# A ring tile for two batches, and a reordered prologue, in a Fourier mixer followed by an expert block

## The chip, the cores and the metric

One core of a Trainium2 chip. The metric is the device time of one execution in microseconds; a time quoted is the median of several runs. The kernel is bound by TensorE (PE) for all but its first 42 us. In the profile's lines PE is TensorE, DVE is VectorE, ACT is ScalarE, POOL is GpSimd ("Pool" in the text) and SP is SyncE; a line starts with the start and the length in us, L265 is line 265 of that run's kernel, and the bracket gives the idle time of the engine before it and what the profile says ended it. "Half clock" means that the granted TensorE clock is 0.5.

## The reference

```python
X = np.fft.rfft(x, axis=1)                    # x: 8 batches x 3008 positions x 256
Y = X * (filt_r + 1j * filt_i)[None]
y = np.fft.irfft(Y, n=3008, axis=1)
h = y.reshape(8 * 3008, 256) @ w_in           # 256 x 2048
out = np.maximum(0.01 * h, h) @ w_out         # 2048 x 256
```

## The kernel before

The transform of 3008 = 94 x 32 points is done as matmuls in two stages each way: S1 (by 94), a transpose T1 on VectorE, S2 (by 32), a product with the filter, SA (inverse of S2), a transpose T2, SB (inverse of S1), which leaves the mixer output with channels on partitions. The expert block runs in 47 chunks of 512 tokens. Batches 1 to 7 are mixed in the shadow of the expert matmuls. Batch 0 has nothing to hide behind: its mixing is the prologue. "The first expert matmul" below is the first one of `moe1_group`.

The two tiles of mixer output and the chunk that straddles a batch boundary:

```python
yts = [cpool.tile([P, NDT, N], FP16, name=f"yt{i}") for i in range(2)]
...
    while t < (ci + 1) * CH:                       # moe1_group
        e = min((ci + 1) * CH, (t // N + 1) * N)   # cut at each batch boundary
        pieces.append((t // N, t % N, t - ci * CH, e - t))
        t = e
    for j in range(2):
        for b, lo, o, ln in pieces:
            for dt in range(NDT):
                nc.tensor.matmul(ph[:, j, ds(o, ln)], w_in_sb[...], yts[b % 2][:, dt, ds(lo, ln)], ...)
```

PSUM tiles are taken in turn: two wide ones (two banks each, kind "ph"), three single ones ("pf"). An S2 group of batch 0 handles `n` values of k1 of one half `hf` of the channels; VectorE or Pool multiplies it by both filters, into y tiles that SA reads:

```python
def bank(kind, n, w):
    of = wide if kind == "ph" else single
    t = of[turn[kind] % len(of)]; turn[kind] += 1
    ...
def first_s2(hf, c, n, on_pool):
    ps = bank("ph", n, DH)
    ...                                # matmuls into ps
    if on_pool:                        # ScalarE copies ps to SBUF, Pool multiplies
        ...
    else:
        y = [ypp.tile([P, n, DH], FP16, tag=f"yw{i}", bufs=2, ...) for i in range(2)]
        for i in range(2):             # by the real filter fa, then by the imaginary fb
            nc.vector.tensor_tensor(y[i][:], ps, fs[i], AL.mult)
def first_sa(hf, c):                   # per four k1: two matmuls into a single bank,
    ps = bank("pf", 4, DH)             # then a ScalarE copy to big[2]
```

The prologue's order from T1 on (program order is each engine's order):

```python
t1_part(0, 0, True)(), t1_part(0, 1, True)()
upper(0)                               # copies of filter halves, ScalarE and VectorE
first_s2(0, 0, 8, False)
first_s2(0, 8, 8, True)
x_load(1)                              # next batch, Pool queue
t1_part(0, 2, True)()
keep_warm(4)                           # filler matmuls on an idle tile
first_s2(0, 16, 4, False)
first_s2(0, 20, 4, True)
t1_part(0, 3, True)()
first_sa(0, 0), first_sa(0, 16)
keep_warm(3)
first_s2(1, 0, 8, False)
first_s2(1, 8, 8, True)
first_sa(0, 8), first_sa(0, 20)
keep_warm(2)
...                                    # load of w_out
first_s2(1, 16, 8, False)
first_sa(1, 0)
keep_warm(4)
first_t2(0), first_t2(1)
first_sa(1, 16), first_sa(1, 8)
first_t2(2), first_t2(3)
```

Before all this Pool's queue gets the loads of x, twelve filter loads, the inverse constants `i1` (wanted by SB) and `w_in`.

## Time and profile before

| | before |
|---|---|
| time, first 3 runs | 783.31 us (783.25 to 783.39) |
| profiled run | 783.91 us, span 782.1 us |
| end of the first two T1 transposes | 20.45 us |
| start of T2 | 34.67 us |
| first expert matmul | 42.48 us |
| PE busy after that, to 771.5 | 728.10 of 729.02 us |

Two quantities matter: how long the chain from T1 to the first expert matmul is (42.48 - 20.45 = 22.03 us), and the PE work after it. I count from the end of T1 because the loads before it land up to a microsecond earlier or later from run to run.

### The profile page before, as it was taken

The numbers are of one execution on the slowest core, as the hardware profiler recorded it, in microseconds if no ns is written. First come the engines' busy times: TensorE is split into PE (matmuls) and PEld (weight loads), VectorE is DVE, ScalarE is ACT, GpSimd is POOL, SyncE is SP. The second block draws the span as 40 slices with busy tenths as digits, with TensorE's granted clock in tenths as the row PEclk, the third lists the DMA queues.
The fourth block names the chain that finished last, engine by engine and source line by source line (L and its number), as shares of the span: only waits on it lengthen the run. The fifth ranks groups of instructions, "written<-read, shape, count | busy, mean of one in ns | idle before, by whom it ended". The sixth has DMA issues, their size and how long they took to land.

```text
span 782.1 us, 13672 instructions
## 1 busy us (share of the span) xinstructions
PE 773.4 (99%) x5844; PEld 531.4 (68%) x5844; DVE 367.3 (47%) x462; ACT 551.2 (70%) x784; POOL 152.3 (19%) x126
## 2 busy tenths in 40 slices
PE   9899999999999999999999999999999999999998
PEld 4366677666776667766777667776677666776666
DVE  3879751865237641577307754087432765200000
ACT  3686769676787767777587775967668776666664
POOL 5963300340004300052001510025000340000000
PEclk9999999999999999999999999999999999999999
DMA  9963102301041101510105010140101001101111
GB/s 179 226 110 73 38 28 56 94 27 42 28 108 41 41 28 41 108 42 28 42 28 121 28 37 32 42 107 28 41 28 41 28 28 41 41 33 35 41 41 54
DMA packets 39387, 44.16 MB, mean 56 GB/s; under 512 B 11266, under 2 KB 37506, under 8 KB 38658
## 3 DMA queue, kind: packets, MB, share of 16 engines
q0 software_dynamic: 13136, 17.78, 13.3%
q1 hardware_dynamic: 26192, 25.53, 9.3%
q8 instruction: 45, 0.74, 0.4%
q14 instruction: 14, 0.11, 0.0%
HBM read 35.67 MB, written 24.64 MB: 77 GB/s over the span
## 4 chain that ended last, share of the span: by engine, by line
PE 94%; DMA 2%; POOL 2%; ACT 1%; DVE 1%; issue 1%; POOLq 0%
PE ph L376 41%; PE po_ps L390 41%; PE pf L176 3%; PE pf L243 2%; PE pf L231 2%; PE pf L216 2%; DMA fb_sb<-in_filt_i_dram 2%; PE pf L390 1%; POOL fy_h_c L276 1%; ACT big L187 0%; POOL x_sb L132 0%; DVE big L297 0%; ACT big L290 0%; POOL fb_sb L140 0%; ACT gt_c L381 0%
## 5 line engine op out<-in xcount | busy, mean ns | idle before, releaser
L381 ACT ACTIVATE gt_c<-ph 128x1024 f16<-128x1024 f32 x376 | 384.8, 1023 | 195.7 <-PE ph L376 194.7
L376 PE MATMUL ph<-yt,w_in_sb 128*128 128x512 f16 (+7 forms) x1728 | 386.7, 351 | 0.3
L390 PE MATMUL po_ps<-w_out_sb,gt_c 128*128 128x256 f16 x2944 | 381.4, 272 | 0.6 <-ACT ost_c_t L397 0.6
L390 PEld LDWEIGHTS <-gt_c 128*128 128x128 f16 x3008 | 290.7, 98 | 87.1 <-issue 1.9
L376 PEld LDWEIGHTS <-w_in_sb 128*128 128x128 f16 x1728 | 162.9, 98 | 94.4 <-issue 0.4
L224 POOL TENSOR_TENSOR y_b_g<-p_b_g,p_b_g 128x512 f16<-128x512 f32 x84 | 106.9, 1272 | 225.4 <-DVE p_b_g L222 225.4
L199 DVE STREAM_TRANSPOSE big<-big 128x1024 f32<-128x1024 f32 x32 | 55.9, 1847 | 126.2 <-ACT big L187 126.2
L187 ACT CAST big<-pf 128x512 f16<-128x512 f32 x186 | 106.6, 604 | 1.7 <-PE pf L256 1.7
L246 DVE CAST yt<-pf 128x376 f16<-128x376 f32 x112 | 56.3, 544 | 86.0 <-PE pf L243 86.0
L220 DVE TENSOR_TENSOR p_b_g<-pf,fa_sb 128x512 f32<-128x512 f32 x84 | 58.1, 692 | 38.1 <-PE pf L216 35.6
L397 ACT COPY ost_c_t<-po_ps 128x256 f32<-128x256 f32 x184 | 69.4, 377 | 6.6 <-PE po_ps L390 5.4
L207 DVE STREAM_TRANSPOSE big<-big 128x1024 f32<-128x1024 f32 x28 | 51.1, 1934 | 34.1 <-ACT big L187 34.1
L221 DVE TENSOR_TENSOR p_b_g<-pf,fb_sb 64x512 f32<-64x512 f32 x84 | 58.2, 692 | 1.1
L222 DVE TENSOR_TENSOR p_b_g<-pf,fb_sb 64x512 f32<-64x512 f32 x84 | 57.4, 683 | 1.1
L132 POOL DMA_DIRECT2D x_sb<-in_x_dram x12 | 6.6, 553 | 253.3 <-PE pf L176 252.5
L243 PEld LDWEIGHTS <-big 128*128 128x128 f16 x448 | 25.6, 98 | 13.2
L176 PE MATMUL pf<-x_sb,f_sb 94*128 94x256 f16 x224 | 33.9, 272 | 0.2 <-DVE yt L246 0.2
L231 PE MATMUL pf<-y_b_g,small_sb 128*128 128x512 f16 x84 | 31.8, 379 | 0.0
L216 PE MATMUL pf<-big,small_sb 128*128 128x512 f16 x84 | 31.8, 379 | 0.0
L243 PE MATMUL pf<-i_sb,big 128*128 128x94 f16 x448 | 28.6, 206 | 0.0
L176 PEld LDWEIGHTS <-f_sb 94*128 94x128 f16 x224 | 20.9, 97 | 9.1 <-issue 0.4
L318 PE MATMUL po_ps<-idle 128*128 128x512 f16 x72 | 19.5, 418 | 1.2 <-DVE one L165 1.2
(46 smaller groups left out, 158.8 us busy)
## 6 DMA issues: line engine op xcount, KB each, us to landing
out_dram<-ost_c_t SPq DMA_DIRECT2D x92, 256.0 KB, 2.1
x_sb<-in_x_dram POOLq DMA_DIRECT2D x6, 1536.0 KB, 11.4
x_sb<-in_x_dram POOLq DMA_DIRECT2D x3, 480.0 KB, 9.8
fa_sb<-in_filt_r_dram POOLq DMA_DIRECT2D x6, 192.0 KB, 10.2
fb_sb<-in_filt_i_dram POOLq DMA_DIRECT2D x6, 192.0 KB, 8.5
w_in_sb<-in_moe_w_in_dram POOLq DMA_DIRECT2D x1, 1024.0 KB, 13.0
w_out_sb<-in_moe_w_out_dram POOLq DMA_DIRECT2D x1, 1024.0 KB, 13.0
x_sb<-in_x_dram POOLq DMA_DIRECT2D x1, 1024.0 KB, 7.9
```

Source lines behind the costliest of these rows:

```text
L176: nc.tensor.matmul(ps[:, j, :], f1_sb[:N1, n2, :], x_sb[:N1, n2, :], start=True, stop=True)
L187: copy(paired(dst)[:, ds(n0, nn), ds(e0, de)], ps.rearrange("p n (e t) -> p n e t", t=2))
L220: nc.vector.tensor_tensor(p1[:], ps, fa, AL.mult)
L221: nc.vector.tensor_tensor(p2[0:64], ps[64:P], fb[64:P], AL.mult)
L222: nc.vector.tensor_tensor(p2[64:P], ps[0:64], fb[0:64], AL.mult)
L224: nc.gpsimd.tensor_tensor(y1[:], p1[:], p2[:], AL.add)
L243: nc.tensor.matmul(ps[:, j, :], src[:, dt, n2, :], i1_sb[:, n2, :], start=True, stop=True)
L246: copy(yv[:, :, ds(4 * h, 4)], ps.rearrange("p c a -> p a c"))
L376: nc.tensor.matmul(ph[:, j, ds(o, ln)], w_in_sb[:, dt, ts(ct, P)], yts[b % 2][:, dt, ds(lo, ln)], start=(dt == 0), stop=(dt == NDT - 1),)
L381: nc.scalar.activation(gts[ci][:, ds(2 * g, 2), :], ph, AF.Lrelu)
L390: nc.tensor.matmul(po, gts[ci][:, ct, ts(tj, P)], w_out_sb[:, ct, :], start=(ct == 0), stop=(ct == NCT - 1))
L397: nc.scalar.copy(ost[:, tj % 2, :], po)
```

## The change

Intent: one tile for two batches, so that half of the straddling chunks need no cut; and a prologue in which Pool multiplies earlier, fewer engines wait on each other, and the load of the constants leaves Pool's queue.

```diff
-    yts = [cpool.tile([P, NDT, N], FP16, name=f"yt{i}") for i in range(2)]
+    yt = cpool.tile([P, NDT, 2 * N], FP16, name="yt")
...
-    nc.gpsimd.dma_start(i1_sb[:], i1_d.ap())
-    nc.gpsimd.dma_start(w_in_sb[:], ...)
...
-        ps = bank("ph", n, DH)
+        ps = bank(two[n // 8], n, DH)          # groups of four: a single bank
...
     t1_part(0, 0, True)(), t1_part(0, 1, True)()
+    nc.vector.memset(i1_sb[:, 0, 0:2], 0.0)    # holds the load back until T1 is done
+    nc.sync.dma_start(i1_sb[:], i1_d.ap())
     upper(0)
+    first_s2(0, 8, 8, True)
+    nc.gpsimd.dma_start(w_in_sb[:], ...)
+    t1_part(0, 2, True)()
     first_s2(0, 0, 8, False)
... (old order removed)
+    keep_warm(3)
+    first_s2(0, 20, 4, True)
+    for n0 in (0, N2 // 2):
+        x_load(1, n0, N2 // 2)
+    t1_part(0, 3, True)()
     first_s2(0, 16, 4, False)
+    first_s2(1, 0, 8, False)
+    first_sa(0, 0)
+    first_s2(1, 8, 8, True)
+    first_sa(0, 16)
+    first_s2(1, 16, 4, False)
+    first_sa(0, 8)
+    ... (load of w_out)
+    first_s2(1, 20, 4, False)
+    first_sa(1, 0), first_sa(0, 20)
     keep_warm(3)
     first_t2(0), first_t2(1)
+    first_sa(1, 16), first_sa(1, 20), first_sa(1, 8)
     first_t2(2), first_t2(3)
...
-            e = min((ci + 1) * CH, (t // N + 1) * N)
+            e = min((ci + 1) * CH, (t // (2 * N) + 1) * 2 * N)
```

More of the change, by code (lines that the diff above doesn't have):

```diff
@@ L158 @@
     filt_load(fb_sb, filt_i, DH, DH, 64)
-    nc.gpsimd.dma_start(i1_sb[:], i1_d.ap())
-    nc.gpsimd.dma_start(w_in_sb[:], moe_w_in.rearrange("(dt p) c -> p dt c", p=P))
     idle = cpool.tile([P, CH], FP16, name="idle")
@@ L244, in go @@
                                  start=True, stop=True)
-            yv = yts[b % 2][:, dt, :].rearrange("p (a c) -> p a c", c=N2)
+            yv = yt[:, dt, ds((b % 2) * N, N)].rearrange("p (a c) -> p a c", c=N2)
             copy(yv[:, :, ds(4 * h, 4)], ps.rearrange("p c a -> p a c"))
@@ L307, in first_sb @@
                                  i1_sb[:, n2, :], start=True, stop=True)
-        yv = yts[0][:, dt, :].rearrange("p (a c) -> p a c", c=N2)
+        yv = yt[:, dt, :N].rearrange("p (a c) -> p a c", c=N2)
         copy(yv[:, :, ds(4 * h, 4)], ps.rearrange("p c a -> p a c"))
@@ L329 @@
     t1_part(0, 0, True)(), t1_part(0, 1, True)()
+    nc.vector.memset(i1_sb[:, 0, 0:2], 0.0)
+    nc.sync.dma_start(i1_sb[:], i1_d.ap())
     upper(0)
+    first_s2(0, 8, 8, True)
+    nc.gpsimd.dma_start(w_in_sb[:], moe_w_in.rearrange("(dt p) c -> p dt c", p=P))
+    t1_part(0, 2, True)()
     first_s2(0, 0, 8, False)
-    first_s2(0, 8, 8, True)
-    x_load(1)
-    t1_part(0, 2, True)()
-    keep_warm(4)
-    first_s2(0, 16, 4, False)
-    first_s2(0, 20, 4, True)
-    t1_part(0, 3, True)()
-    first_sa(0, 0), first_sa(0, 16)
-    keep_warm(3)
-    first_s2(1, 0, 8, False)
-    first_s2(1, 8, 8, True)
-    first_sa(0, 8), first_sa(0, 20)
-    keep_warm(2)
-    nc.gpsimd.dma_start(w_out_sb[:], moe_w_out.rearrange("(ct p) d -> p ct d", p=P))
-    first_s2(1, 16, 8, False)
-    first_sa(1, 0)
-    keep_warm(4)
+    keep_warm(3)
[3 more added lines that the diff above has]
+    t1_part(0, 3, True)()
+    first_s2(0, 16, 4, False)
+    first_s2(1, 0, 8, False)
[4 more added lines that the diff above has]
+    first_sa(0, 8)
+    nc.gpsimd.dma_start(w_out_sb[:], moe_w_out.rearrange("(ct p) d -> p ct d", p=P))
+    first_s2(1, 20, 4, False)
+    first_sa(1, 0), first_sa(0, 20)
+    keep_warm(3)
     first_t2(0), first_t2(1)
-    first_sa(1, 16), first_sa(1, 8)
+    first_sa(1, 16), first_sa(1, 20), first_sa(1, 8)
     first_t2(2), first_t2(3)
@@ L368, in moe1_group @@
         while t < (ci + 1) * CH:
-            e = min((ci + 1) * CH, (t // N + 1) * N)
-            pieces.append((t // N, t % N, t - ci * CH, e - t))
+            e = min((ci + 1) * CH, (t // (2 * N) + 1) * 2 * N)
+            pieces.append((t % (2 * N), t - ci * CH, e - t))
             t = e
@@ L373, in moe1_group @@
             ct = 2 * g + j
-            for b, lo, o, ln in pieces:
+            for lo, o, ln in pieces:
                 for dt in range(NDT):
@@ L377, in moe1_group @@
                         ph[:, j, ds(o, ln)], w_in_sb[:, dt, ts(ct, P)],
-                        yts[b % 2][:, dt, ds(lo, ln)],
+                        yt[:, dt, ds(lo, ln)],
                         start=(dt == 0), stop=(dt == NDT - 1),
```

## The prediction

> **What bounds the kernel now.** I read the page first, then a table of stretches cut where the first and the last expert matmul lie, then the order of time of each engine in the first 43 us.
>
> ```profile
> PE 773.4 (99%) x5844; PEld 531.4 (68%) x5844; DVE 367.3 (47%) x462; ACT 551.2 (70%) x784; POOL 152.3 (19%) x126
> PE   9899999999999999999999999999999999999998
> ...
> 0.00:42.48 42.48, 38.21 (x269) 18.87 (x269) 26.79 (x30) 22.33 (x36) 32.03 (x35) 1.00 1.24 201
> 42.48:771.50 729.02, 728.10 (x5513) 506.35 (x5513) 340.49 (x433) 526.75 (x743) 120.27 (x92) 1.00 0.17 48
> 771.50:782.10 10.60, 7.13 (x66) 6.15 (x63) 0.00 (x0) 2.08 (x6) 0.00 (x0) 0.94 0.21 74
> ```
>
> The last three lines are stretches in us: length, busy PE, weight loads, DVE, ACT and Pool with counts, granted clock, DMA share, GB/s. From 42.48 us on TensorE is busy for 728.10 of 729.02 us: only fewer or shorter matmuls help there. The first 42.48 us are a prologue that makes the mixer output of batch 0; its busy PE is largely filler (L318, 72 matmuls on an idle tile). So two numbers decide: the PE work after 42.48 us, and when the first expert matmul (L376) starts.
>
> The prologue by engine, the lines that carry the argument (start, length, engine; in brackets the idle time before and its releaser):
>
> ```profile
> 20.32 1.45 POOL L140 DMA_DIRECT2D fb_sb<-in_filt_i_dram  x1 [0.36 <-DMA fb_sb<-in_filt_i_dram]
> 21.76 0.58 POOL L159 DMA_DIRECT2D i_sb<-inv_const  x1
> 22.47 0.72 POOL L160 DMA_DIRECT2D w_in_sb<-in_moe_w_in_dram  x1
> 23.29 2.29 POOL L276 TENSOR_TENSOR fy_h_c<-fx_h_c,fa_sb 128x512 f16<-128x512 f32 x2
> ...
> 29.69 1.21 DVE L281 TENSOR_TENSOR fy_h_c<-ph,fb_sb 128x1024 f16<-128x1024 f32 x1
> 32.40 1.23 DVE L281 TENSOR_TENSOR fy_h_c<-ph,fa_sb 128x1024 f16<-128x1024 f32 x1 [1.49 <-PE ph L265]
> 33.54 1.21 DVE L281 TENSOR_TENSOR fy_h_c<-ph,fb_sb 128x1024 f16<-128x1024 f32 x1
> 34.67 2.36 DVE L297 STREAM_TRANSPOSE big<-big 128x1024 f32<-128x1024 f32 x2
> 37.38 1.25 DVE L297 STREAM_TRANSPOSE big<-big 128x1024 f32<-128x1024 f32 x1 [0.35 <-ACT big L290]
> ```
>
> Pool can't multiply until it has issued the loads (21.76 to 23.19). DVE later waits 1.49 us for PE, which stands in order behind a product of Pool. After the second pair of T2 transposes (end 39.76) come 64 small matmuls (2.5 us), an eviction of 0.55 us, and the experts.
>
> The DMA engines matter too. Stretches again:
>
> ```profile
> 21.00:26.00 5.00, 4.22 (x15) 1.37 (x14) 4.82 (x6) 1.99 (x4) 4.78 (x6) 1.00 1.82 179
> 26.00:28.50 2.50, 2.15 (x8) 0.71 (x7) 1.44 (x2) 1.30 (x3) 2.48 (x4) 1.00 1.37 330
> ```
>
> From 13.5 to about 26 us they move 179 to 182 GB/s without a gap: the filters, in packets of 256 B, one per engine every 22 ns (some 357 in each half microsecond over 16 engines, counted in the trace's packets). The last filter load is issued at 20.32 and lands 8.5 us later, at 28.8; the next in the same queue, the inverse constants (752 KB in 6016 B packets), issued at 21.76, lands 8.8 us later, at 30.6. They are wanted only at 37.08 (L306).
>
> **What the skill says.** "TensorE: Matmul & The Clock Gate", Back-to-back issue gap, puts a warm matmul at N / 2.4 plus about 2.5 ns. The trace agrees: a group of four 512-column matmuls takes 863 ns from its start to the next group's, one of eight split matmuls with the same columns 873 ns (the usual values), thus 2.5 ns for each extra one. "DMA: Bandwidth & Descriptors", Specifications, gives 512 B as the least transfer for full rate: the filters' 256 B run at 180 GB/s where the mix with the constants reaches 330. The same page, Queues, rings and completion order, lets an engine alternate between queues by packet of several descriptors. Here the trace is finer: between 4.5 and 6 us both queues start equal numbers of data packets (33 of 5120 B, 33 of 2048 B), one for one. "PSUM — Partial Sum Buffer", Specifications (TRN2), gives 8 banks per partition. By the code the program holds all 8 (two wide tiles of two, three single, one tile for outputs and filler), so groups moved into the single banks must share them; what that costs no run shows yet.
>
> **The change part by part.** *Ring tile.* With both batches in one tile the token chunk across an odd boundary (batches 1, 3, 5, 7) is contiguous; boundaries 2, 4 and 6 still wrap. Each such chunk loses 16 x 2 matmuls, so 4 x 32 = 128 of 1728.
>
> ```profile
> L376 PE MATMUL ph<-yt,w_in_sb 128*128 128x512 f16 x1280 | 328.7, 379 | 0.3
> L376 PE MATMUL ph<-yt,w_in_sb 128*128 128x448 f16 x64 | 15.7, 353 | 0.0
> L376 PE MATMUL ph<-yt,w_in_sb 128*128 128x64 f16 x64 | 7.1, 193 | 0.0
> ```
>
> The means (379, 353, 193 ns) contain latency that overlaps, so they must not be subtracted. The 10 ns per group count: 4 chunks x 8 groups x 10 ns = 0.32 us, all on PE. At chunk 5 the merged matmul needs the last mixer eviction of batch 1 (about 117.0) and starts at 117.65: no wait.
>
> *Prologue.* Pool is free after the filter issue at 21.77. The group for Pool now comes first on PE, so ACT's copies start about 21.6 (before 22.42), and Pool's first product at about 22.2 instead of 23.29. Four products at 1.12 end at 26.7; the input weights' issue (0.7) follows, two products to 29.7, two issues for the next batch (1.1), and its last four products 30.9 to 35.4. Before, they ended at 35.09: Pool gives back what it won.
>
> *Inverse constants.* The tiny memset lets SyncE issue them just after the two transposes, at about 20.6, so data flows from 21.5, now in another queue, while the filters still flow. Per engine 8 packets of 6016 B at some 222 ns (1.8 us landing to landing above) put 1.8 us between the filters' packets. The last filter then lands at 28.8 + 1.8 = 30.6, not 28.8.
>
> *DVE.* Filter copy to 21.5, T1 to 22.7, group (0,0) to 25.0, T1 to 26.1, (0,16) to 27.3. Group (1,0) has its matmuls at 27.2, multiplies by the real filter once that has landed (26.6 + 1.8 = 28.4), and by the imaginary one from 30.65 to 31.9. Then (1,16) until 33.0. Groups of four share the three single banks with the inverse stage. Counting turns from the code (four in the first stage, then on), (1,20) gets the bank of (1,16), and the later inverse group (0,20) gets that of (1,20). So (1,20): matmul 33.07, 0.6 long, two products to 34.95; then inverse (0,20): two matmuls 0.6, ACT's copy 0.65, and only at 36.25 can T2 start (34.67 before). Four transposes in two pairs of 2.38 end at 41.0 (before 39.76). The other 64 small matmuls take 2.6 us from 38.7, so the second half begins at 41.3 instead of 39.81, and the experts at 43.95 instead of 42.48: +1.47 us. Sum: 783.31 + 1.47 - 0.32 = 784.46.
>
> **Rivals.** (a) The constants don't hinder the filters, or only after (1,0) has them: (1,0) ends at 30.1, (1,16) at 31.2, (1,20) at 33.2, T2 starts 34.5 and ends 39.2, thus -0.55 with -0.32: 782.4. For it: DVE no longer waits for Pool's short group, and the author gated the load by hand. Against it: the engines' full share until 26 us, and the one-for-one alternation. (b) Pool's products bind instead: the last inverse copies end at 36.5 and T2's second pair at 38.9, so 782.1, where (a) would hold without the bank wait. (c) One tile makes the tracker order evictions of one batch behind reads of the other: some 0.3 us in each of 8 slots of 7 batches, 800 us. Against it: before, ACT writes one half of `big` (35.22 to 37.35) while DVE transposes the other (34.67 to 37.03), so halves of one tile run side by side. (d) The weights, asked for after 26.7, come late. The bytes ahead of them are the same, so they land at about 35.5 as before (22.47 + 13.0), well ahead of 42. The next batch's load keeps its landing of 42.7, and its first half comes about 3.6 us earlier.
>
> **Range and chances.** I give my sum about seven in ten and (a) or (b) three; the weighted middle lies a little under the sum, 784.2 us, and 782.2 to 785.2 holds both. Two per cent would be 15.7 us; only (c) comes near.
>
> **What would show it.** 1600 instead of 1728 matmuls at L376; the first of them near 43.9 us; the last filter landing near 30.6 and the constants near 24; DVE idle before the imaginary product of (1,0), and T2 beginning near 36.3, released by ACT's copy of inverse group (0,20). I am wrong if filters land by 29 us, or T2 starts by 34.6; then the experts start before 42.2 and the time is near 782.4.

## The result, and the profile after

The kernel after took 785.91 us (784.87 to 788.45, 6 runs), the kernel before in the same rounds 783.35 us (783.18 to 783.98, 6 runs). The ratio is 1.0035, 95% interval 1.002 to 1.0049. A ratio is the mean time of one kernel's runs over that of the other's of the same rounds, so not quite the ratio of the medians. The time lies 0.7 us above the stated range.

Busy time and the expert matmuls of the kernel after, from its page:

```profile
PE 772.7 (99%) x5709; PEld 524.0 (67%) x5709; DVE 367.9 (47%) x465; ACT 551.3 (70%) x784; POOL 151.4 (19%) x126
...
L379 PE MATMUL ph<-yt,w_in_sb 128*128 128x512 f16 (+3 forms) x1600 | 386.4, 366 | 0.3
```

There are 1600 expert matmuls instead of 1728. I matched the 376 expert evictions of both traces: the offset between them falls by 0.08 us at each of chunks 5, 17, 29 and 41 (10 ns per group) and moves by a few hundredths elsewhere in the steady part. That is the 0.32 us of the ring tile. The loss is in the prologue, but for 0.11 us that PE loses at the seventh and eighth eviction of chunk 0 (0.13 in e9, the same kernel again) and 0.16 us behind the last expert eviction; what causes these two I have not looked for. The prologue's order of time in the kernel after:

```profile
19.87 0.34 SPq L330 DMA_DIRECT2D i_sb<-inv_const  x1
...
28.02 1.22 DVE L279 TENSOR_TENSOR fy_h_c<-ph,fa_sb 128x1024 f16<-128x1024 f32 x1 [1.09 <-PE pf L287]
...
30.11 1.22 DVE L279 TENSOR_TENSOR fy_h_c<-ph,fb_sb 128x1024 f16<-128x1024 f32 x1 [0.87 <-PE pf L287]
...
32.58 0.59 PE L263 MATMUL pf<-big,small_sb 128*128 128x512 f16 x1 [0.92 <-DVE fy_h_c L279]
...
33.86 0.69 DVE L279 TENSOR_TENSOR fy_h_c<-pf,fa_sb 128x512 f16<-128x512 f32 x1 [1.33 <-PE pf L287]
...
35.20 0.60 PE L287 MATMUL pf<-fy_h_c,small_sb 128*128 128x512 f16 x2 [1.17 <-DVE fy_h_c L279]
...
36.48 2.37 DVE L295 STREAM_TRANSPOSE big<-big 128x1024 f32<-128x1024 f32 x2 [1.33 <-ACT big L288]
...
44.29 1.31 PE L379 MATMUL ph<-yt,w_in_sb 128*128 128x512 f16 x4
```

Four waits stand in a row. The imaginary product of group (1,0) at 30.11 waits 0.87 us. The matmul of (1,20) at 32.58 waits for the products of (1,16) to leave its bank. The products of (1,20) at 33.86 wait, long after that matmul has ended (33.17). Inverse group (0,20) at 35.20 waits for (1,20) to leave its bank; ScalarE's copy of it releases T2 at 36.48. From T1's end (19.81) to the first expert matmul the chain takes 24.48 us instead of 22.03, 2.45 us more. The span grew by 1.8 us only, because in this run x landed earlier and T1 ended 0.64 us sooner; the ring tile's 0.32 us were nearly lost again in the 0.11 and 0.16 us above.

What the first of these waits for: the profile names PE. The load's own landing says more. This is the answer for the last filter load of the kernel after, issued at 19.62:

```profile
DMA to landing us min/median/max: 10.4/10.4/10.4
```

19.62 + 10.4 = 30.02: the filter lands at 30.0 and the product starts at 30.11. A matmul of the inverse stage happened to end at 30.1 as well, so the name of the releaser is the latest event, not the cause. In e9, the same kernel again, the profile names the filter itself ahead of this product (0.94 us, DMA fb_sb). The packets agree: from 24.0 to 25.5 us the queue of the filters and that of the constants start 92 and 95 data packets, one for one, so the 6016-byte packets of the constants hold back the 256-byte ones of the filters, which before went at some 350 per half microsecond.

Something I had not looked for stands in the table of stretches of the kernel after (columns as in the prediction; the third from the end is the granted clock):

```profile
24.00:28.00 4.00, 2.19 (x6) 0.80 (x7) 2.92 (x4) 0.41 (x1) 3.98 (x5) 0.85 1.47 271
28.00:32.00 4.00, 3.55 (x10) 1.13 (x9) 3.12 (x4) 3.25 (x7) 3.99 (x6) 0.72 1.14 198
```

PE idles 2.55 us ahead of group (1,0), and from 26.8 us its clock is half for 3.4 us. In the kernel before it stays at 1.00 in the whole prologue. The Trainium skill, "TensorE: Matmul & The Clock Gate", Part 1, tells of this gate: a free-running window of 3.4 us, and half clock after an idle window. The traces agree on the length: in each of the 16 kept ones all changes of the clock are multiples of 3.413 us apart. They differ on what "idle" takes. Here are two neighbouring windows of that grid in the kernel after, then one of e11 and one of e6 (experiments below):

```profile
23.43:26.84 3.41, 1.03 (x3) 0.34 (x4) 3.41 (x5) 0.02 (x1) 3.39 (x4) 1.00 1.38 305
26.84:30.25 3.41, 3.41 (x9) 1.18 (x8) 1.45 (x3) 2.02 (x4) 3.40 (x5) 0.50 1.45 186
...
20.69:24.11 3.42, 1.78 (x5) 0.40 (x4) 3.24 (x4) 1.07 (x2) 3.20 (x4) 1.00 1.82 179
...
29.14:32.55 3.41, 1.95 (x7) 0.60 (x6) 2.41 (x3) 2.69 (x5) 3.33 (x5) 1.00 1.07 214
```

Behind the first and the third the clock fell, behind the fourth (1.95 us of busy PE) it did not. It is so in every window of the 16 traces: all 23 falls came behind a window with 1.78 us of busy PE or less, and no window with 1.95 us or more was followed by one. Where the grid lies against the program differs from run to run (its first edge stands 4.2 to 7.1 us from the start), so the same idle time can fill one window in one run and be shared by two in the next.

### The profile page after: what moved, and what is told of

The parts are those of the page before. It is cut to its first block, busy times and chain, and to the rows that moved or that the text cites. A ratio compares the mean times of both kernels' runs of the same rounds, so it can differ in the third digit from the quotient of the medians.

```text
span 783.9 us, 13411 instructions
## 1 busy us (share of the span) xinstructions
PE 772.7 (99%) x5709; PEld 524.0 (67%) x5709; DVE 367.9 (47%) x465; ACT 551.3 (70%) x784; POOL 151.4 (19%) x126
## 4 chain that ended last, share of the span: by engine, by line
PE 94%; DVE 1%; ACT 1%; issue 0%; DVEq 0%
PE ph L379 41%; PE po_ps L393 41%; PE pf L174 3%; PE pf L241 2%; PE pf L229 2%; PE pf L214 2%; PE pf L393 1%; DVE fy_h_c L279 1%; PE pf L287 0%; ACT big L185 0%; DVE big L197 0%; PE ph L304 0%; DVE big L295 0%; ACT gt_c L384 0%; PE ph L263 0%
## 5 line engine op out<-in xcount | busy, mean ns | idle before, releaser
L379 PE MATMUL ph<-yt,w_in_sb 128*128 128x512 f16 (+3 forms) x1600 | 386.4, 366 | 0.3
L379 PEld LDWEIGHTS <-w_in_sb 128*128 128x128 f16 x1600 | 154.5, 98 | 95.7 <-issue 0.4
L316 PE MATMUL po_ps<-idle 128*128 128x512 f16 x65 | 17.9, 426 | 1.2 <-DVE one L163 1.2
## 6 DMA issues: line engine op xcount, KB each, us to landing
fb_sb<-in_filt_i_dram POOLq DMA_DIRECT2D x6, 192.0 KB, 10.4
```

Of the source, the lines that this page charges most:

```text
L379: nc.tensor.matmul(ph[:, j, ds(o, ln)], w_in_sb[:, dt, ts(ct, P)], yt[:, dt, ds(lo, ln)], start=(dt == 0), stop=(dt == NDT - 1),)
```

## The experiments

Each experiment was timed in five rounds against the kernel before on the same chip; the kernels of one group (e1 to e4, e5 to e8, e9 to e12, e13 and e14) shared a chip. The last column is read from each one's trace.

| run | time us (range) | before | ratio (95%) | T1 end to first expert matmul |
|---|---|---|---|---|
| before | | | | 22.03 |
| after | 785.91 (784.87 to 788.45) | 783.35 | 1.0035 (1.0020 to 1.0049) | 24.48 |
| e1 ring only | 783.15 (782.67 to 783.76) | 783.53 | 0.9995 (0.9984 to 1.0007) | 22.02 |
| e2 prologue only | 787.10 (785.36 to 788.73) | 783.53 | 1.0046 (1.0033 to 1.0059) | 26.38 |
| e3 constants by SyncE, old order | 784.24 (783.38 to 784.81) | 783.53 | 1.0008 (0.9996 to 1.0020) | 22.95 |
| e4 constants behind the filters | 784.09 (783.42 to 784.53) | 783.53 | 1.0006 (0.9993 to 1.0019) | 23.63 |
| e5 constants late by SyncE | 788.63 (787.42 to 789.08) | 783.43 | 1.0064 (1.0052 to 1.0076) | 26.90 |
| e6 own y buffers | 784.94 (784.71 to 787.57) | 783.43 | 1.0032 (1.0018 to 1.0045) | 24.11 |
| e7 other bank | 784.64 (784.42 to 785.21) | 783.43 | 1.0017 (1.0005 to 1.0029) | 23.33 |
| e8 one long filler | 787.99 (785.57 to 788.77) | 783.43 | 1.0053 (1.0041 to 1.0065) | 27.14 |
| e9 after again | 786.36 (785.17 to 789.15) | 783.40 | 1.0046 (1.0029 to 1.0063) | 24.50 |
| e10 fillers in all waits | 785.93 (785.26 to 786.60) | 783.40 | 1.0033 (1.0021 to 1.0045) | 25.41 |
| e11 before without fillers | 783.27 (782.57 to 783.99) | 783.40 | 1.0000 (0.9988 to 1.0013) | 21.64 |
| e12 mended | 783.74 (783.07 to 785.54) | 783.40 | 1.0008 (0.9996 to 1.0020) | 22.43 |
| e13 mended, fewer fillers | 782.71 (782.48 to 783.09) | 783.48 | 0.9990 (0.9978 to 1.0003) | 21.16 |
| e14 ring, no fillers | 783.38 (782.89 to 784.24) | 783.48 | 1.0001 (0.9988 to 1.0015) | 21.86 |

### e1 and e2: which half of the change

e1 is the kernel before with the ring tile's lines alone; e2 is the kernel after with the two old tiles.

> The kernel before with the ring tile alone. My theory: it saves 10 ns in each of 32 groups, 0.32 us, and touches nothing else: 783.0 us beside 783.35, 1600 matmuls in the expert line, and eviction offsets that fall by 0.08 us at chunks 5, 17, 29 and 41. Rival: the one tile brings waits in the main part; then this run is slower than before.

> The kernel after with the two old tiles, so the new prologue alone. My theory: the whole loss lies here, and it is 0.3 us slower than the kernel after: about 786.2 us. Rival (part of the loss comes from the ring tile): clearly under 785.9.

e1 came out 0.4 us faster, with the same prologue (22.02 us); its interval includes 1, but its trace from the first expert matmul to the end is 0.35 us shorter. e2 came out slower still than the kernel after, and 0.9 us over what I expected (three of its six runs have clock 0.996), so the whole loss is the new prologue. Its profiled run has a second stretch of half clock, now late in the prologue:

```profile
36.00:40.00 4.00, 4.00 (x14) 1.58 (x13) 2.37 (x2) 1.76 (x4) 4.00 (x1) 0.66 1.07 221
```

### e3: the moved load alone, in the old order

```diff
-    nc.gpsimd.dma_start(i1_sb[:], i1_d.ap())
...
     t1_part(0, 0, True)(), t1_part(0, 1, True)()
+    nc.vector.memset(i1_sb[:, 0, 0:2], 0.0)
+    nc.sync.dma_start(i1_sb[:], i1_d.ap())
```

> The kernel before with only the inverse constants moved to SyncE behind the memset. If the delay of the filters (1.9 us) costs by itself in any order, about 784.3 us or more. If it costs only where VectorE is ready for the filters early, as in the new order, then the old order hides it behind the 1.5 us that VectorE idles for PE anyway, and Pool starts 0.6 us earlier: 782.8 to 783.4 us. The last filter must land about 10.4 us after its issue instead of 8.5.

The first of the two outcomes came, not the hiding: the median is 0.7 us higher, and though the interval of the ratio still includes 1, the trace shows the chain 0.92 us longer (22.95 us instead of 22.03). VectorE's order of time:

```profile
30.85 1.23 DVE L280 TENSOR_TENSOR fy_h_c<-ph,fb_sb 128x1024 f16<-128x1024 f32 x1 [1.12 <-DMA fb_sb<-in_filt_i_dram]
33.19 1.23 DVE L280 TENSOR_TENSOR fy_h_c<-ph,fa_sb 128x1024 f16<-128x1024 f32 x1 [1.11 <-PE ph L264]
```

Here the profile names the filter itself as what ended the wait at 30.85 (it landed 10.5 us after its issue, before 8.5). I had thought the old order's slack behind it would absorb that. But the next group's matmuls need the wide tile of this one, so they could start only after 32.1, and the slack was gone. So the moved load alone hurts either order.

### e4 and e5: the same load, out of the filters' way

e4 puts the constants back in Pool's queue, ahead of `w_in` and thus behind all filters. e5 keeps SyncE, but moves memset and issue behind `first_s2(1, 0, 8, False)`.

> The kernel after with the constants back in Pool's queue, just ahead of the input weights, thus behind all filters. My theory: the last filter lands 8.5 us after its issue, the imaginary product of group (1,0) starts right after the real one (about 1.0 us earlier), and all that follows moves by as much: 784.9 us. Rival (the filters are not what it waited for; the inverse stage or y buffers are): no change, 785.9 us.

> The kernel after with the memset and the SyncE issue moved behind the products of group (1,0). My theory: the filters are not hindered, so the imaginary product of (1,0) starts about 1.0 us earlier, as with the constants behind the filters in Pool's queue: about 784.1 us. The constants then land about 36 us, before the small matmuls want them. Rival: the queue itself (SyncE instead of Pool) is what costs; then no gain over 785.9.

In e4 the last filter lands 8.5 us after its issue, and the imaginary product follows the real one at once:

```profile
27.97 1.23 DVE L279 TENSOR_TENSOR fy_h_c<-ph,fa_sb 128x1024 f16<-128x1024 f32 x1 [0.95 <-PE pf L287]
29.11 1.22 DVE L279 TENSOR_TENSOR fy_h_c<-ph,fb_sb 128x1024 f16<-128x1024 f32 x1
```

The chain is 0.85 us shorter than in the kernel after, near the 1.0 expected. The median fell by more, 1.8 us: from the first expert matmul to the end this trace is 0.49 us shorter too, which no part of the theory explains, and none of its runs is a slow one of low clock (0.997 to 0.998 in all), while the one in the kernel after (0.993) lifts that median by 0.2; some 0.3 us stay open. The real product here waits 0.95 us for inverse group (0,0), whose y buffers it takes over and whose four matmuls ran at half clock (1.61 us, in e10 at full clock 1.04). In e5 the filters are as free as in e4, and T2 starts 15.58 us after T1's end instead of 16.67. But the constants, issued at 30.8 into engines that now carry the weights and the next batch, land 10.9 us later, and PE waits for them:

```profile
41.78 0.68 PE L304 MATMUL pf<-i_sb,big 128*64 128x94 f16 x16 [3.76 <-DMA i_sb<-inv_const]
```

So e5's theory for the filters holds (its rival, that SyncE itself costs the filters, does not), my "about 36 us" for the landing was wrong by almost 6 us, and the PE idle after that drew another half-clock stretch at 42.4. Right behind the filters, in the same queue (e4), the constants hinder neither.

### e6 and e7: the two waits behind (1,0)

```diff
 e6: -  y = [ypp.tile([P, n, DH], FP16, tag=f"yw{i}", bufs=2, ...)
     +  y = [ypp.tile([P, n, DH], FP16, tag=f"yw{i}" if n == 8 else "y", bufs=2 if n == 8 else 4, ...)
 e7: -  ps = bank(two[n // 8], n, DH)
     +  ps = bank("ph" if (hf, c) == (1, 20) else two[n // 8], n, DH)
```

> The kernel after with the products of the groups of four in the four small y buffers of the main part, so that the fifth VectorE group no longer waits until the inverse stage has read the buffers of the third. My theory: group (1,20) multiplies at 33.2 instead of 33.86 and all behind it moves by 0.65 us: 785.2 us. Rival (only the bank counts): 785.9.

> The kernel after with group (1,20) in a wide PSUM tile, so that it does not wait for the bank of (1,16), nor the inverse group (0,20) for its own. My theory: its products follow at once (32.5), and T2 starts 2.5 us earlier or more; the whole then is about 783.2 us, no slower than the kernel before. Rival (the late filters alone make the loss): about 785.5.

VectorE in e6:

```profile
30.14 1.22 DVE L279 TENSOR_TENSOR fy_h_c<-ph,fb_sb 128x1024 f16<-128x1024 f32 x1 [1.23 <-DMA fb_sb<-in_filt_i_dram]
...
33.24 0.69 DVE L279 TENSOR_TENSOR fy_h_c<-pf,fa_sb 128x512 f16<-128x512 f32 x1 [0.68 <-PE pf L263]
```

From the imaginary product of (1,0) to the first product of (1,20) it takes 3.10 us, in the kernel after 33.86 - 30.11 = 3.75: the 0.65 us are the y buffers. The releaser is now the group's own matmul (L263) and no longer the inverse stage (L287). The buffers are two per filter; (1,20) is the fifth VectorE group and takes that of the third, (1,0), which inverse group (1,0) must have read. Its runs at clock 0.998 took 784.71 to 784.94, two at 0.996 took 787.5.

In e7 T2 starts 15.53 us after T1's end instead of 16.67, so the chain is 1.14 us shorter, not the 2.5 I expected. (The filter came 0.5 us later after T1's end in this run; counted from the imaginary product of (1,0), as for e6, the bank was worth 1.64 us, 4.73 instead of 6.37.)

```profile
33.70 1.46 PE L287 MATMUL pf<-fy_h_c,small_sb 128*128 128x512 f16 x6 [0.61 <-DVE fy_h_c L279]
34.54 0.69 DVE L279 TENSOR_TENSOR fy_h_c<-ph,fa_sb 128x512 f16<-128x512 f32 x1 [0.90 <-PE pf L287]
```

With (1,20) out of the turn, inverse group (1,0) gets the bank of (1,16) and waits at 33.70, and (1,20)'s products wait for that through the y buffers. What the move did win is that inverse (0,20) no longer waits for (1,20). Shared buffers in turn pass a wait on; one fix shows the next.

### e8, e9 and e10: the clock

e8 adds `keep_warm(11)` ahead of `first_s2(1, 0, 8, False)`. e9 is the kernel after unchanged. e10 adds to e8 `keep_warm(8)` ahead of `first_s2(1, 20, 4, False)` and `keep_warm(5)` ahead of `first_sa(0, 20)`.

> The kernel after with 11 more filler matmuls (2.4 us) ahead of group (1,0), where TensorE idles 2.55 us and its granted clock then falls to half for 3.4 us. If the half clock is on the path that ends the prologue, the time falls by 0.3 us or more and the runs draw together (785.5 or less, all within 0.8 us, clock 0.999 or more). If it only slows matmuls that wait anyway, the median stays at 785.9, though the outlier of 788 may go.

> The kernel after, unchanged, to have its runs on the same chip as the next three: about 785.9 us. If the half clock is what scatters it, its slower runs have the lower mean clock (one window of 3.4 us at half clock lowers the mean by 0.002), and each window that falls late in the prologue adds 1 to 3 us.

> The kernel after with filler matmuls in every long wait of TensorE in the prologue (11 ahead of group (1,0), 8 ahead of (1,20), 5 ahead of inverse group (0,20)), each no longer than its wait. My theory: no window of half clock before the experts, clock 0.999 to 1.0, runs within 1 us of each other, at about 785.4 us: the fillers take away the scatter and the slow tail, and the late filters and the two waits stay. Rival (the waits, not the clock, scatter): the runs scatter as before.

e8 is the worst place for a cure: it kept the clock up to 33 us, then PE idled (1.94 us busy in the four from 28 us), and two half-clock windows fell on the end of the prologue:

```profile
32.00:36.00 4.00, 2.29 (x5) 0.52 (x4) 2.04 (x4) 1.18 (x2) 3.60 (x4) 0.65 1.07 221
36.00:40.00 4.00, 3.93 (x10) 1.46 (x11) 2.25 (x3) 1.19 (x2) 3.80 (x1) 0.50 1.06 219
```

Four of its runs (clock 0.995 or 0.996) took 787.4 to 788.8; the one whose clock was 1.0 took 785.57. The twelve runs of the kernel after (with e9) fall the same way: eight at 0.998 took 784.87 to 786.33, one at 0.996 took 787.28, three at 0.993 took 788.45 to 789.15. In e10 the clock was 1.0 in all runs and they lie within 1.34 us (e9: 3.98):

```profile
32.00:36.00 4.00, 2.89 (x12) 0.99 (x10) 2.67 (x5) 1.10 (x2) 3.82 (x4) 1.00 1.06 218
36.00:40.00 4.00, 3.63 (x22) 1.56 (x23) 2.46 (x4) 2.70 (x5) 3.75 (x1) 1.00 1.09 225
```

So the slow tail goes with the clock, and the rest of the loss does not: e10 is still 2.5 us over the kernel before. Five runs without a slow one are not much beside four slow in twelve, but the grid of windows agrees: in the kernel after a window that starts between 31.4 and 32.1 us holds 1.8 us of busy PE or less (in e9 30.8 to 31.7), so about a quarter of the positions of the grid bring a late fall (an estimate from these two traces), and in the prologue of e10 the emptiest such window, wherever it starts after 8 us, holds 2.3 us. The mean clock alone does not tell: it also holds the half clock behind the last matmul (in the kernel before from 780.7 us), and a run of e7 with 0.996 took 784.64, no more than its others.

Its median did not reach the 785.4 I expected; its filters came late as well (the imaginary product 11.24 us after T1's end, in the kernel after 10.30). That is the far end of a scatter: in the seven traces with this load (after, e2, e6 to e10) it lies between 10.30 and 11.24. Why it scatters I have not explained.

### e11: too few fillers in the old order

> The kernel before without the 13 fillers of its second stage (4, 3, 2 and 4). If too few fillers let the clock fall, half-clock windows appear and the time rises by 0.5 to 3 us with scatter, with nothing of the change in it. If the fillers were idle ballast, the time stays at 783.4.

The clock did fall, for 3.4 us from 24.1, but the time did not rise (783.27), and the chain is even 0.39 us shorter. So half clock costs where PE's matmuls are on the path that ends the prologue, and early in S2, where VectorE and Pool set the pace, it cost nothing. Nor did it slow the S2 matmuls themselves: L265 took 595 ns each inside that stretch and 602 after it, while the inverse ones (L289) took 630 and 380. My expectation of 0.5 to 3 us was wrong.

### e12, e13 and e14: a version without the causes

e12 takes from the kernel after: the constants of e4, the buffers of e6, the bank of e7. It also puts inverse (0,20) ahead of (1,0), the second half of the next batch's load behind Pool's last products, and fillers in the waits. e13 removes some of these fillers:

```diff
-    keep_warm(4)
     first_s2(1, 20, 4, False)
     first_sa(0, 20), first_sa(1, 0)
-    keep_warm(3)
+    keep_warm(2)
     first_t2(0), first_t2(1)
     first_sa(1, 16), first_sa(1, 20)
-    keep_warm(4)
+    keep_warm(3)
     first_sa(1, 8)
```

> The kernel after with the constants in Pool's queue behind the filters, group (1,20) in a wide tile, groups of four in the small y buffers, inverse group (0,20) ahead of (1,0), the second half of the next batch's load behind Pool's last products, and fillers in the waits. If the late filters, the bank, the y buffers and the clock together are the whole loss, the new order now does what it was meant to: Pool's last product sets the end, T2's second pair starts about 16.0 us after T1's end (before: 16.9), and with the ring tile the time is about 782.3 us, under the 783.4 of before. If something else is wrong with the new order, it stays over 783.4.

> The mended order of the run before, without its 4 fillers ahead of (1,20), and with 2 and 3 instead of 3 and 4 behind: there they stood on the path (inverse group (1,8) began 0.65 us after Pool's last product). If those fillers were the rest of the loss, T2's second pair starts about 16.1 us after T1's end instead of 17.4, the second expert matmul about 21.7 us after it (before: 22.5), and the time is about 782.3 us. If the new order can't beat the old one for another reason, it stays at 783.4 or over.

> The old prologue without its 13 fillers, with the ring tile: the two small gains that single runs showed, 0.32 us and about 0.3 us, added: about 782.8 us beside 783.4. If the fillers' removal was within noise, 783.1.

e12 missed. Its T2 started early, but PE's order of time shows my own fillers on the path:

```profile
34.83 1.03 PE L316 MATMUL po_ps<-idle 128*128 128x512 f16 x4
...
35.69 1.03 PE L287 MATMUL pf<-fy_h_c,small_sb 128*128 128x512 f16 x4
```

Pool's last product was done at about 35.0; inverse (1,8) waited for the fillers until 35.69. Another part of the miss lies outside the program: 1.9 to 2.7 us of e12's times are not in the core's span, in the other runs 1.7 to 2.1; by the spans (median 781.4 us) e12 is no slower than the kernel before (781.6). In e13:

```profile
34.50 1.06 PE L287 MATMUL pf<-fy_h_c,small_sb 128*128 128x512 f16 x4
...
36.28 2.37 DVE L295 STREAM_TRANSPOSE big<-big 128x1024 f32<-128x1024 f32 x2 [1.25 <-ACT big L288]
```

T2's second pair starts 16.13 us after T1's end (expected 16.1), the second expert matmul 21.70 us after it (expected 21.7), and the time is 782.71 us (expected 782.3) against 783.48, all five runs within 0.61 us. Its interval just includes 1, so the timing alone does not settle that it is faster; the trace shows a chain 0.87 us shorter and the ring tile's 0.32. e14 stayed within noise of the kernel before, so the timing tells neither the ring tile nor the fillers' removal; its trace has the ring tile's 0.36 us behind the first expert matmul, and a half-clock stretch from 24.1 us like e11's.

## Why the prediction was right or wrong

Right:
- **Ring tile.** 128 matmuls fewer, 0.32 us saved, at the four chunks named, no new wait (trace of the kernel after; e1).
- **Constants against filters.** By their counts both queues alternate packet for packet; the last filter was predicted at 10.2 us after T1's end (30.65 - 20.45) for the product it releases and came at 10.3. e4 shows the product free of the wait when the load is out of the way, and e3 shows the longer chain without the rest of the change. The start of the constants was wrong and did no harm: predicted about 1 us after T1's end, landing near 24, they started at 23.7, 3.9 us after it, and landed at 26.5; the filters still had packets left to be held back.
- **The bank.** (1,20) waits for (1,16), inverse (0,20) for (1,20). The rivals (a) and (b), which would have made it faster, did not occur. T2 was to start 15.80 us after T1's end and started at 16.67; the first point below has the difference.
- Pool gave back what it won: its last products ended at 34.7, 14.9 us after T1's end; before 14.6.

Wrong: the time, by 1.45 us against the sum (784.46) and 1.7 against the number. The step that failed is the one for group (1,20).
- **"matmul 33.07, 0.6 long, two products to 34.95" for group (1,20).** The prediction let the products follow their matmul at once. It walked the turns of the PSUM banks and left out those of the y buffers, two deep, which the fifth VectorE group must wait for. Against T1's end the first product came 0.80 us later than that step has it (14.05 for 13.25 us), and 0.70 of this arose after (1,0)'s imaginary product. e6 measures the wait at 0.65 us. With 0.07 until T2 and 0.11 behind it, the chain grew by 2.45 us where the prediction said 1.47. That is 0.98 of the 1.45 us.
- **What followed the first expert matmul** was taken as unchanged but for the ring tile: 0.27 us were lost there (0.11 in chunk 0, 0.16 behind the last eviction), cause open. In the profiled run T1's early end (0.64 us) is made up by the profiled run before being 0.60 us over 783.31, so 784.46 + 0.98 + 0.27 gives its 785.71.
- **The clock was taken as constant.** The new order has fewer fillers and longer PE waits. The early half-clock stretch, which nearly all runs have, costs little in the kernel after, where the late filter binds meanwhile. In some runs the mean clock is lower still, and they are 1.8 to 3.7 us above the middle of the others (785.50); the traces of e2 and e8 show such further stretches on SA, that of e5 one on SB. Of the six runs behind the result one is of this kind and lifts the median by 0.2 us, to 785.91. So the clock makes the tail and is not why the time lies outside the range.
- The weighting added to it. Seven to three of 784.46 and 782.1 to 782.4 gives 783.8, not 784.2; either way it pulled the number below a sum that was already too low.

Open: why the filters' landing scatters by 0.9 us, the 0.27 us behind the first expert matmul, and where between 1.78 and 1.95 us of busy PE in a window of 3.41 the clock's limit lies.

## What to carry to other kernels

A load moved to another queue to spare an issue slot still shares the engines: ask what is in flight, and what waits for it. When work is reordered, walk every rotating buffer, SBUF as well as PSUM, with its new turn; the count of a turn can make a wait between two groups that have nothing to do with each other. And a prologue with long PE waits has a clock of its own: look at the granted clock by stretches, cut at its own changes, count the busy PE in the worst window that could be cut there, and put fillers where they are shorter than the wait.

## What the Trainium skill lacked or had wrong

- "DMA: Bandwidth & Descriptors", Queues, rings and completion order, has an engine drain a packet of some 9 to 17 descriptors from one queue before the next. Here the trace's data packets start one for one by their counts (it does not tell the engines apart): 92 of 256 B and 95 of 6016 B between 24.0 and 25.5 us in the kernel after.
- The same page, Specifications, gives about 0.6 us to the first byte for a load issued by SyncE. The constants, issued at 19.87 us into engines full of filter packets, started their first data packet at 23.7 us, 3.9 us later, and landed 6.6 us after issue; issued at 30.8 beside larger packets (e5) they took 10.9 us.
- "TensorE: Matmul & The Clock Gate" advises against PE gaps over about 3 us. In the kernel after a gap of 2.55 us, which left 1.03 us of busy PE in a window of 3.41, was followed by 3.4 us of half clock, and in e11 one of 1.64 us with 1.78 us busy. No page tells how much work in a window is enough: in these traces 1.78 us was too little and 1.95 us enough.
- No page gives a figure for the cost of a moving operand read in 4-byte pieces. In the kernel before the S2 matmuls of batch 0, which read so, took 602 ns each (L265), the inverse ones with contiguous rows and as many columns 380 ns (L289); at half clock in e11 595 and 630 ns.
